# An mLSTM cell with a GELU layer behind it, on one core: the place of one weighing of values and of the sums of w_out

## The chip, the cores and the metric

The kernel runs on one core of a Trainium2 chip. A core has five engines that run side by side, each through its own list of instructions in order: TensorE (PE) multiplies matrices, VectorE (DVE), ScalarE (ACT) and GpSimd (POOL) work element by element, and SyncE (SP) issues the transfers (DMAs). An engine waits for another only where a semaphore says so. The metric is the device time of the program in microseconds; smaller is better.

## What is computed

Two blocks follow each other. The first is an mLSTM cell over 4 batches, 8 heads, 768 steps and a head dimension of 40; the second takes its result as 3072 tokens of 320 features through a hidden layer of 2048.

```python
for t in range(S):
    m_new = maximum(f[t] + m, i[t])
    C = exp(f[t] + m - m_new) * C + exp(i[t] - m_new) * outer(v[t], k[t])
    n = exp(f[t] + m - m_new) * n + exp(i[t] - m_new) * k[t]
    m = m_new
    y[t] = sigmoid(o[t]) * (C @ q[t]) / max(|n . q[t]|, 1)
x = y as (tokens, heads * head_dim)
h = x @ w_in
out = (0.5 * h * (1 + erf(h / sqrt(2)))) @ w_out
```

## The kernel before

**Chunks.** The 768 steps are cut into six chunks of 128. Within a chunk the recurrence becomes matrix products: scores of keys and queries, multiplied by a matrix W of gate weights, times the values; what comes from earlier chunks is carried in a state of each batch. A chunk of all four batches is 512 tokens, and its second block (up: x times w_in, then GELU; down: times w_out) is computed while the cell of the next chunk runs.

**Order.** The program is written out by hand as words. `FRONT` is the order of the first chunk's cell, its up and its down and of the second chunk's cell. Then a loop makes passes c = 1 to 5: `up(g, sums_too, turns)` for chunk c, and then `play(DOWN, steps)`, in which the down of chunk c (words F) and the cell of chunk c + 1 are mixed. Every engine executes its own instructions in the order in which these words issue them, so a word's place is its place in each queue. Words have a letter and a batch: M masks the weights' exponents on POOL, W takes the exponential on ACT, G is the output gate, S the scores (PE) and their product with W (DVE, line 458), C the carried part and the state's update, V the values (PE line 515), Y finishes y, X turns y for the next up (PE line 550), R splits it in two parts of fewer bits, K and Q turn keys and queries on DVE, L loads the fourth batch's blocks, Z takes the next step of a list called `later`, and N is a late sum.

**Finishing a y.** `finish(b)` (Y) multiplies the read state by the gated output on POOL (line 528) from the third chunk on, makes a denominator on DVE (lines 530 to 532), and multiplies y by its reciprocal on DVE (line 533), which needs POOL's product. The last 64 columns are then copied twice by DVE (`y_rest`, line 539) for the transposes on PE.

**Weighing values.** `weigh_values(b)` (line 442) multiplies the values of a batch by their decays. From the third chunk on it runs on POOL. It is called in `turn_q`, so directly behind the turning of the batch's queries. Only the state's update (`carry`, PE line 474) reads it.

**Down as seven products.** From the second chunk on, down is a two by two block product in Strassen's manner, in seven products instead of eight. It needs four sums of blocks of w_out: T1 = B12 - B11, T2 = B22 - T1, T3 = B22 - B12 and T4 = B21 - T2, each over 8 slices of 128x160 (`weight_sum`, line 624: one step is two subtractions on DVE). T1 and T2 lie in w_sums; T3 is written over B12 in w_out; T4 goes into three buffers that up used before. They are made once, in pass 1. The hidden layer's own sums (`hidden_sums`, lines 642 to 644) are made on DVE in each pass.

**Up.** `up` takes four pairs of hidden rows. A weight of w_in is split into a high part (ACT, line 606) and a low part (DVE, line 608), and `join_weight` (line 614) makes their difference; `split_to` and `join_weight` are no-ops once a weight is there, as in later passes. `out` is the GELU on ACT (line 725). `turns` are the K and Q of two batches of the next cell.

Of the kernel before, what the change touches and what calls it, by code (L numbers as in the profile page):

```python
# [31 lines left out]
    C2 T3 J K Y1 U U J S3 V2 C3 K J K K J J F K F F F J K J X0 K K J F R0 F F J F K G3 Y2 F J K V3 J K F K X1 J  # L32
    J R1 F F F F K X2 B8 J R2 F Y3 Z Z X3 R3 B9 B10 F"""
DOWN = """
    M0 Z M1 W0 F L3 F W1 Z Z F S0 Z S1 K2 C0 M2 Z C1 G0 G1 G2 G3 V0 Z V1 W2 Z M3 F Q2 K3 Q3 Y0 F F W3 F Z S2 S3
    C2 C3 V2 V3 F N F Y1 X0 R0 Y2 F F Y3 X1 R1 F X2 R2 F X3 R3 F"""


# [1 line left out]
def kernel(  # L40
# [18 lines left out]
    B, H, S, D = q.shape  # L59
    L = P  # L60
    NCH = S // L
# [76 lines left out]
    def load_blocks(n, to):  # L138

        c, b = divmod(n, B)  # L140
        for i, src in enumerate((k, q)):
            for d, w in ((0, 32), (32, D - 32)):
                for g in range(4):
                    t = c * L + 32 * g
                    nc.sync.dma_start(out=to[64 * i + d:64 * i + d + 32, :, 32 * g:32 * g + w],
                                      in_=src[b, :, t:t + 32, d:d + w].rearrange("h t d -> t h d"))
# [204 lines left out]
    class Cell:  # L351
# [63 lines left out]
        def turn_q(self, b):  # L415
            self.turn_half(b, 1)
            n = self.c * B + b + (1 if b < B - 2 else 2)
            if b < B - 1 and n < NCH * B:
                load_blocks(n, by_block)
            if self.c < NCH - 1:  # L420
                self.weigh_values(b)

# [171 lines left out]
    def split_weight():  # L594
        i = len(w_lo)
        if i in (0, 3, 5, 8):
            two = shared([P, NX, 2, WP // 2], F32R, "w_in_hi")
            w_hi.extend([two[:, 0], two[:, 1]])
        elif i == 2:
            two = shared([P, 2, 2, WP // 2], F32R, "w_rest_hi")  # L600
            w_hi.append(two[:, 0])
            rest_two.append(two[:, 1])
        elif i == 7:
            w_hi.append(rest_two[0])
        w = w_all[i]
        nc.scalar.activation(out=w_hi[i], in_=w, func=AF.Copy, scale=PART * 2.0 ** -12)
        w_lo.append(w_f(F32R, "w_in_lo"))
        nc.vector.scalar_tensor_tensor(out=w_lo[i], in0=w_hi[i], scalar=-BASE * 2.0 ** 12, in1=w, op0=OP.mult, op1=OP.add)
# [3 lines left out]
    def join_weight(i):  # L612
        w_mid[i] = raw.tile([P, 2, WP // 2], F32R, name="w_in_mid", tag="pow") if i % 5 in (1, 4) else w_f(F32R, "w_mid")
        nc.vector.tensor_tensor(out=w_mid[i], in0=w_hi[i], in1=w_lo[i], op=OP.add)  # L614

    def weight_sum(n):
        x, y = {1: (Bm[0][1], Bm[0][0]), 2: (Bm[1][1], T[1]), 3: (Bm[1][1], Bm[0][1])}.get(n) or (Bm[1][0], T[2])
        if n == 4:

            parts = [raw.tile([P, 3, HD], F32, name="t4", tag=tag) for tag in ("sig", "pow", "sig")]  # L620
            T[4] = lambda j: parts[j // 3][:, j % 3, :]

        def step(j):
            nc.vector.tensor_tensor(out=T[n](j), in0=x(j), in1=y(j), op=OP.subtract)

        return [lambda j=j: (step(j), step(j + 1)) for j in range(0, HF, 2)]
# [10 lines left out]
    def hidden_sums(g, f0, f1):  # L637

        (a11, a21), (_, a22) = [[g.t[:, HF * e + f0:HF * e + f1, HT * h:HT * (h + 1)] for h in range(2)]
                                for e in range(2)]  # L640
        s1, s2 = [t[f0 // (HF // 2)][:, f0 % (HF // 2):f0 % (HF // 2) + f1 - f0, :] for t in (g.s1, g.s2)]
        nc.vector.tensor_tensor(out=s1, in0=a21, in1=a22, op=OP.add)  # L642
        nc.vector.tensor_tensor(out=s2, in0=s1, in1=a11, op=OP.subtract)  # L643
        nc.vector.tensor_tensor(out=a21, in0=a11, in1=a21, op=OP.subtract)
# [44 lines left out]
    def up(g, sums_too, turns):  # L689

        def split_to(i):
            while len(w_lo) <= i:
                split_weight()

        def pair(f, ahead):

            at = [f // 2 * 5 + f % 2 * 3 + x for x in range(NX)]
            split_to(at[1])
            for i in at:
                if i not in w_mid:  # L700
                    join_weight(i)
            pus = [[pool.tile([P, TG], F32, name="pu", tag=tag) for e in range(2)]
                   for pool, tag in (((ps_h, "h"), (ps_mm, "a")), ((ps_tr, "tr"), (ps_mm, "b")))[f % 2]]
            ahead()
            mid = [w_mid.pop(i) for i in at]
            for n, (w, x) in enumerate((([w_hi[i] for i in at], parts["x"]), ([w_lo[i] for i in at], parts["x_lo"]), (mid, parts["x_all"]))):
                for i in range(2):
                    for e in range(2):
                        for k in range(NX):
                            nc.tensor.matmul(pus[i][e], w[k][:, e, i * P:(i + 1) * P], x[:, k, :],  # L710
                                             start=(n == 0 and k == 0), stop=False, skip_group_check=True)
            return pus

        def rest(u, banks, order):
            mid = w_mid.pop(5 * u + 2)
            for i in order:
                pu = banks[i]
                for n, (w, x) in enumerate(((w_hi[5 * u + 2], parts["x"]), (w_lo[5 * u + 2], parts["x_lo"]), (mid, parts["x_all"]))):
                    for e in range(2):
                        r = halves[e]  # L720
                        nc.tensor.matmul(pu[e], w[r, i // 2, i % 2 * P:(i % 2 + 1) * P], x[r, NX, :], start=False,  # L721
                                         stop=(n == 2), skip_group_check=True)

        def out(i, e, pu):
            nc.scalar.activation(out=g.t[:, HF * e + i, :], in_=pu[e], func=AF.Gelu, scale=4097.0)  # L725

        b0 = pair(0, lambda: split_to(4))
        b1 = pair(1, lambda: join_weight(2))
        for step in turns[:1]:
            step()  # L730
        rest(0, b0 + b1, (0, 1, 2, 3))
        split_to(6)
        join_weight(5)
        join_weight(6)
        for i, pu in enumerate(b0 + b1):
            for e in range(2):
                out(i, e, pu)
        b2 = pair(2, lambda: split_to(9))
        hidden_sums(g, 0, 2)
        hidden_sums(g, 2, 4)  # L740
        b3 = pair(3, lambda: join_weight(7))
        for step in turns[1:] + sums_too:
            step()
        rest(1, b2 + b3, (2, 3, 0, 1))
        for i, e in ((2, 0), (2, 1), (3, 0), (0, 0), (1, 0), (3, 1), (0, 1), (1, 1)):
            out(4 + i, e, (b2 + b3)[i])
        hidden_sums(g, HF - 2, HF)
        hidden_sums(g, HF - 4, HF - 2)
# [96 lines left out]
    def in_turn(steps):  # L845
        todo = list(steps)
        return lambda: todo.pop(0)() if todo else None

    def cell_steps(c, letters, before=None):
        cell = Cell(c)  # L850
        cell.before = before
        return dict(zip(letters, (cell.mask, cell.weights, cell.gate, cell.turn, cell.scores, cell.carry, cell.values,
                                  cell.finish, cell.turn_y, cell.split_x, cell.load_last, cell.turn_k,
                                  cell.turn_q)))

    first_g = Hidden(False)
    n_pieces = range(len(pieces))
    steps = dict(P=fetch, L=lambda n: load(n, 0, 2), O=lambda n: load(n, 2, 4), B=load_M, E=second_gates, N=later_gates,
                 I=keep_clock, D=lambda: decays_turned(0, 2, 0, 1), Q=lambda: decays_turned(2, NCH - 1, 1, NCH - 1),
                 A=in_turn(first_up_steps(0)), U=in_turn(first_up_steps(1)), F=in_turn(first_down_steps(first_g)),  # L860
                 K=in_turn(lambda i=i: conv_one(i) for i in n_pieces), H=products_begin,
                 J=in_turn(lambda i=i: conv_two(i) for i in n_pieces), Z=split_weight)
    steps |= cell_steps(0, "mwgtscvyx") | cell_steps(1, "MWGTSCVYXR")
    play(FRONT, steps)
    for c in range(1, NCH):
        g, later, steps = Hidden(True), [], {}
        if c + 1 < NCH:
            steps = cell_steps(c + 1, "MWGTSCVYXRLKQ", g)
        up(g, weight_sum(1) + weight_sum(2) if c == 1 else [], [lambda b=b: (steps["K"](b), steps["Q"](b)) for b in range(2)] if steps else [])
        if c == 1:  # L870
            later = weight_sum(3) + weight_sum(4)
        products, late = down_steps(c, g)
        steps |= dict(F=in_turn(products), Z=in_turn(later), N=late)
        play(DOWN if c + 1 < NCH else "F " * 14, steps)
# [30 lines left out]
```

## Time and profile before

| What | Value |
|---|---|
| Median of 6 runs | 491.39 us (489.97 to 494.62) |
| The profiled execution: device time | 493.81 us |
| The profiled execution: span from first to last instruction | 492.0 us |
| PE busy | 473.4 us, 96% of the span |
| DVE busy | 346.9 us, 71% |
| ACT busy | 222.8 us, 45% |
| POOL busy | 70.9 us, 14% |
| Mean granted clock of PE | 0.990 |

Times inside the profile are microseconds from the span's first instruction. An engine's timeline gives, for each group of like instructions, the start, the length of the group, the engine, the line, the operation, what it writes and reads, and how many there are; in brackets stands how long the engine sat idle before it and what ended the wait. A group's length counts from the start of its first to the end of its last instruction. Instructions of one engine can overlap by a little[...]. The stages of interest are up and down of pass 1 (135.5 to 164.5 and 164.5 to 212.1) and, for comparison, those of pass 2 (212.1 to 240.6 and 240.6 to 285.1).

### The profile page before, as it was taken

What the parts mean: (1) busy time and instruction counts of PE and PEld (TensorE: products, weight loads), DVE (VectorE), ACT (ScalarE), POOL (GpSimd) and SP (SyncE); (2) the same over time, 40 slices, a digit from 0 to 9 for tenths busy, and PEclk for the clock granted to TensorE, in tenths of its full rate; (3) what the DMA queues carried; (4) which work ended last, traced back from release to release, by engine and by line L of the source; (5) the groups of instructions that cost most, each with busy time, mean ns of one, the idle gap of its engine ahead of it and who ended that gap; (6) DMA issues with size and microseconds to landing.
All of it is one profiled execution on the core that took longest, in us unless ns stands there. A gap on an engine that the chain in (4) does not pass through costs nothing.

```text
span 492.0 us, 10730 instructions
## 1 busy us (share of the span) xinstructions
PE 473.4 (96%) x4184; PEld 412.8 (84%) x4184; DVE 346.9 (71%) x727; ACT 222.8 (45%) x477; POOL 70.9 (14%) x108
## 2 busy tenths in 40 slices
PE   3899999999999998999999999999999999999997
PEld 2687888877677898987899987899987899977996
DVE  7689787989877997956577856487857387724321
ACT  7595999845434762113672113672103762212300
POOL 3001120000100125400035400036000113000000
PEclk9599999999999999999999999999999999999999
DMA  6979954338561246832237932246931240000001
GB/s 115 238 182 197 243 124 95 104 108 179 105 152 14 31 87 107 168 80 28 27 61 130 172 87 22 28 84 110 177 82 20 31 87 8 28 27 1 1 0 55
DMA packets 164434, 44.24 MB, mean 90 GB/s; under 512 B 154176, under 2 KB 157408, under 8 KB 164384
## 3 DMA queue, kind: packets, MB, share of 16 engines
q1 hardware_dynamic: 164384, 43.56, 45.0%
q8 instruction: 33, 0.54, 0.5%
q14 instruction: 17, 0.14, 0.1%
HBM read 39.52 MB, written 4.01 MB: 88 GB/s over the span
## 4 chain that ended last, share of the span: by engine, by line
PE 80%; DVE 9%; ACT 4%; DMA 2%; issue 2%; POOL 1%; SPq 0%; DVEq 0%; POOLq 0%
PE po L784 28%; PE pu L710 21%; PE po L761 7%; PE pu L721 6%; PE pu L655 4%; PE ps L455 4%; PE ph L515 3%; PE pf L479 2%; PE pf L474 1%; ACT W L390 1%; PE px L550 1%; PE pu L661 1%; DMA bits<-in_moe_w_in_dram 1%; DMA W<-M_d 1%; DVE ob L533 1%
## 5 line engine op out<-in xcount | busy, mean ns | idle before, releaser
L784 PE MATMUL po<-w_out,g 128*128 128x160 f32 x640 | 91.2, 300 | 0.0
L725 ACT ACTIVATE g<-pu 128x512 f32<-128x512 f32 x80 | 40.8, 614 | 108.1 <-PE pu L721 108.0
L784 PEld LDWEIGHTS po<-w_out,g 128*128 128x128 f32 x640 | 87.8, 190 | 1.8 <-ACT g L725 1.8
L390 ACT ACTIVATE W<-W,aT 128x128 f32<-128x128 f32 x160 | 48.8, 389 | 3.6 <-POOL W L364 3.5
L784 PE MATMUL po<-w_sums,sums 128*128 128x160 f32 x320 | 47.5, 302 | 0.0
L784 PEld LDWEIGHTS po<-w_sums,sums 128*128 128x128 f32 x320 | 44.2, 190 | 0.7 <-DVE sums L643 0.3
L560 ACT ACTIVATE x_hi<-px 128x384 fp32r<-128x384 f32 x20 | 9.8, 490 | 75.8 <-PE px L550 75.8
L458 DVE TENSOR_TENSOR W<-ps,W 128x512 f32<-128x512 f32 x48 | 30.2, 682 | 17.1 <-ACT W L390 11.8
L710 PE MATMUL pu<-x_hi,w_in_hi 128*128 128x512 f32 x160 | 41.4, 401 | 0.0
L710 PE MATMUL pu<-x_lo,w_in_lo 128*128 128x512 f32 x160 | 40.6, 395 | 0.0
L364 POOL TENSOR_SCALAR_AFFINE_SELECT W<-W 128x1024 f32<-128x1024 f32 x20 | 22.6, 1135 | 103.5 <-DMA W<-M_d 92.4
L642 DVE TENSOR_TENSOR sums<-g 128x512 f32<-128x512 f32 x20 | 13.8, 688 | 33.3 <-ACT g L725 33.3
L710 PEld LDWEIGHTS pu<-x_hi,w_in_hi 128*128 128x128 f32 x160 | 29.4, 188 | 8.2 <-ACT g L725 1.9
L710 PEld LDWEIGHTS pu<-x_lo,w_in_lo 128*128 128x128 f32 x160 | 30.1, 188 | 7.2
L761 PE MATMUL po<-w_out,g 128*128 128x320 f32 x128 | 35.7, 434 | 0.0
L710 PE MATMUL pu<-x_all,w_in_mid 128*128 128x512 f32 x80 | 31.7, 396 | 0.1
L710 PE MATMUL pu<-x_all,w_mid 128*128 128x512 f32 x80 | 31.7, 396 | 0.0
L761 PEld LDWEIGHTS po<-w_out,g 128*128 128x128 f32 x128 | 23.8, 190 | 9.3
L797 DVE TENSOR_TENSOR o_sb<-po,o_sb 128x320 f32<-128x320 f32 (+1 forms) x27 | 12.5, 464 | 26.9 <-PE po L784 23.0
L614 DVE TENSOR_TENSOR w_in_mid<-w_in_hi,w_in_lo 128x512 fp32r<-128x512 f32 x20 | 14.6, 732 | 21.6 <-PE pu L710 21.6
L655 PE MATMUL pu<-first_x,w_in 128*128 128x256 f32 x128 | 28.8, 381 | 0.5 <-DVE W L458 0.5
L402 POOL MEMSET g<- 32x1024 f32 x8 | 7.6, 945 | 148.1 <-ACT W L390 117.6
(166 smaller groups left out, 882.9 us busy)
## 6 DMA issues: line engine op xcount, KB each, us to landing
W<-M_d SPq DMA_DIRECT2D x20, 512.0 KB, 5.3
bits<-in_moe_w_in_dram SPq DMA_DIRECT2D x20, 256.0 KB, 5.0
bits<-in_moe_w_out_dram SPq DMA_DIRECT2D x16, 320.0 KB, 3.1
ob<-in_o_gate_dram SPq DMA_DIRECT2D x24, 160.0 KB, 3.8
out_dram<-o_sb SPq DMA_DIRECT2D x24, 160.0 KB, 1.9
vb<-in_v_dram SPq DMA_DIRECT2D x22, 160.0 KB, 5.4
kb<-in_k_dram SPq DMA_DIRECT2D x22, 160.0 KB, 5.0
blocks<-in_k_dram SPq DMA_DIRECT2D x48, 32.0 KB, 2.2
```

The costliest lines, as they stand in the source:

```text
L364: nc.gpsimd.affine_select(out=t, in_=t, compare_op=OP.is_ge, fill=1.0e30, base=0, pattern=[[0, H], [1, L]], channel_multiplier=-1)
L390: nc.scalar.activation(out=W[n][:, h, :], in_=src, func=AF.Exp, scale=-1.0, bias=aT[:, self.c, r:r + 1])
L455: nc.tensor.matmul(ps[hip][:, p, :], kT[r, p, :], qT[r, p, :], start=True, stop=True)
L458: nc.vector.tensor_tensor(out=w, in0=ps[hip], in1=w, op=OP.mult)
L515: nc.tensor.matmul(ph[r, h, :], Pm[:, h, r], vb[turn_of(n)][:, h, :], start=True, stop=True)
L614: nc.vector.tensor_tensor(out=w_mid[i], in0=w_hi[i], in1=w_lo[i], op=OP.add)
L655: nc.tensor.matmul(banks[-1][e][:, i - i0, :], in_tile(i, x)[:, e, i % 2 * P:(i % 2 + 1) * P], first_x[:, x, t0:t1], start=(x == 0 and i = ...
L710: nc.tensor.matmul(pus[i][e], w[k][:, e, i * P:(i + 1) * P], x[:, k, :], start=(n == 0 and k == 0), stop=False, skip_group_check=True)
L721: nc.tensor.matmul(pu[e], w[r, i // 2, i % 2 * P:(i % 2 + 1) * P], x[r, NX, :], start=False, stop=(n == 2), skip_group_check=True)
L725: nc.scalar.activation(out=g.t[:, HF * e + i, :], in_=pu[e], func=AF.Gelu, scale=4097.0)
L761: nc.tensor.matmul(po[b], g.t[:, f, b * L:(b + 1) * L], w_out[:, f, :], start=(f == 0), stop=(f == NF - 1))
L784: nc.tensor.matmul(bank[at][:, i, :], lhs(j, t), rhs(j), start=(first and i == 0 and j == 0), stop=(i == n - 1 and j == HF - 1), skip_grou ...
```

## The change

It has two parts.

The first takes the fourth batch's `weigh_values(3)` out of `turn_q` and gives it a word of its own, D3, which stands in `DOWN` behind Y0, the finishing of the first y. On POOL, the weighing of the fourth batch's values and the multiplication of the first y change places. This concerns passes 1, 2 and 3; the cell of the last chunk weighs nothing.

The second moves the sums of w_out in pass 1. Before, T1 and T2 (8 steps, 16 subtractions) were made in `up`, behind the turning of the second batch's keys and queries, and T3 and T4 (8 steps) in the words Z of `DOWN`. Now five steps (all of T1 and the first of T2) stand ahead of the third pair of hidden rows, directly behind the GELUs of the first two pairs; the other three steps of T2 and the four of T3 stand where T1 and T2 stood; and only T4's four steps are left for the words Z, of which they take the first four. The number of instructions of each kind stays the same on every engine.

```diff
 DOWN = """
-    M0 Z M1 W0 F L3 F W1 Z Z F S0 Z S1 K2 C0 M2 Z C1 G0 G1 G2 G3 V0 Z V1 W2 Z M3 F Q2 K3 Q3 Y0 F F W3 F Z S2 S3
+    M0 Z M1 W0 F L3 F W1 Z Z F S0 Z S1 K2 C0 M2 Z C1 G0 G1 G2 G3 V0 Z V1 W2 Z M3 F Q2 K3 Q3 Y0 D3 F F W3 F Z S2 S3
...
             if b < B - 1 and n < NCH * B:
                 load_blocks(n, by_block)
+            if self.c < NCH - 1 and b < B - 1:
+                self.weigh_values(b)
+
+        def weigh_last(self, b):
             if self.c < NCH - 1:
                 self.weigh_values(b)
...
                 out(i, e, pu)
+        for step in sums_too[:5]:
+            step()
         b2 = pair(2, lambda: split_to(9))
         hidden_sums(g, 0, 2)
         hidden_sums(g, 2, 4)
         b3 = pair(3, lambda: join_weight(7))
-        for step in turns[1:] + sums_too:
+        for step in turns[1:] + sums_too[5:]:
             step()
...
-            steps = cell_steps(c + 1, "MWGTSCVYXRLKQ", g)
-        up(g, weight_sum(1) + weight_sum(2) if c == 1 else [], [lambda b=b: (steps["K"](b), steps["Q"](b)) for b in range(2)] if steps else [])
+            steps = cell_steps(c + 1, "MWGTSCVYXRLKQD", g)
+        up(g, weight_sum(1) + weight_sum(2) + weight_sum(3) if c == 1 else [], [lambda b=b: (steps["K"](b), steps["Q"](b)) for b in range(2)] if steps else [])
         if c == 1:
-            later = weight_sum(3) + weight_sum(4)
+            later = weight_sum(4)
```

## The prediction

> **What bounds the kernel now.** The page's table of engines has TensorE (PE) busy for 473.4 of 492.0 us, and 80% of the chain that ended last is PE: a change pays only where PE waits. So I asked next for the busy time by stage. The windows view, cut where the chain shows PE passing from up to down, gives for pass 1 (two rows, up and down) and pass 2 (two rows), in columns stretch, PE, weight loads, VectorE (DVE), ScalarE (ACT), GpSimd (POOL), clock, DMA share, GB/s:
>
> ```profile
> 135.50:164.50 29.00, 28.89 (x146) 21.98 (x144) 23.23 (x39) 11.96 (x22) 1.10 (x1) 1.00 0.35 72
> 164.50:212.10 47.60, 45.51 (x557) 43.94 (x558) 41.64 (x98) 21.14 (x50) 16.97 (x22) 1.00 0.62 111
> 212.10:240.60 28.50, 28.50 (x146) 22.01 (x144) 16.16 (x25) 6.05 (x12) 0.00 (x0) 1.00 0.23 34
> 240.60:285.10 44.50, 44.50 (x559) 43.82 (x558) 34.33 (x72) 21.18 (x51) 16.84 (x22) 1.00 0.64 114
> ```
>
> Pass 2's down does the same matmuls in 44.5 us with PE never idle; pass 3 is the same (44.4). Pass 1's takes 47.6, and DVE is 7.3 us busier there: mainly 16 of the 32 subtractions that make the sums of w_out. By the chain's starts the stages are 47.65 (164.48 to 212.13) and 44.45 (240.63 to 285.08): **3.20 us is all that pass 1's down can give back**, and the later passes can give nothing.
>
> The timeline of PE shows where the 3.20 lies (start, length, instruction, idle before it):
>
> ```profile
> 191.56 0.32 PE L515 MATMUL ph<-vb,W 128*64 128x41 f32 x4 [0.91 <-DVE W L458]
> 192.16 2.21 PE L515 MATMUL ph<-vb,W 128*64 128x41 f32 x60 [0.28 <-DVE W L458]
> 207.12 0.33 PE L550 MATMUL px<-ident,y_rest 128*128 128x128 f32 x1 [0.81 <-DVE y_rest L539]
> ```
>
> Part by part against pass 2, from the chain: to the second pair of scores 21.96 against 21.67, 0.29 more (the waits list it as po L784 for sums L643, 0.3); scores to the end of values (ph) 7.93 against 6.05, **1.88** more (two rows above); ph to the next up 17.76 against 16.73, 1.03 more (third row and the restart). Sum 3.20.
>
> Why DVE is late for W, in the timelines of DVE and POOL:
>
> ```profile
> 178.11 0.56 DVE L624 TENSOR_TENSOR t<-w_out,w_sums 128x160 f32<-128x160 f32 x2
> ...
> 189.11 0.49 DVE L533 TENSOR_TENSOR ob<-ob,den 128x320 f32<-128x320 f32 x1 [2.00 <-POOL ob L528]
> 189.63 0.23 DVE L539 COPY y_rest<-ob 128x128 f32<-128x128 f32 x1
> 189.78 1.12 DVE L624 TENSOR_TENSOR t<-w_out,w_sums 128x160 f32<-128x160 f32 x2
> 190.82 2.47 DVE L458 TENSOR_TENSOR W<-ps,W 128x512 f32<-128x512 f32 x4
> ```
>
> ```profile
> 185.89 0.74 POOL L442 TENSOR_TENSOR vw<-vb,ewT 128x328 f32<-128x328 f32 x1
> 187.58 0.74 POOL L442 TENSOR_TENSOR vw<-vb,ewT 128x328 f32<-128x328 f32 x1 [0.95 <-DMA vb<-in_v_dram]
> 188.27 0.81 POOL L528 TENSOR_TENSOR ob<-far,ob 128x320 f32<-128x320 f32 x1
> ```
>
> Two causes: POOL weighs the fourth batch's values (second vw), waits 0.95 us for their DMA, and only then multiplies the first y that DVE stands waiting for; and DVE carries subtractions between its other work.
>
> **D3, the fourth batch's values behind the first y.** POOL runs the same instructions, two of them swapped, in passes 1, 2 and 3; SyncE's queue and its DMAs keep their order. The y multiply (ob L528) has its inputs from 180.2 on (far L523), so it follows the first vw: 186.65 to 187.46 instead of 188.27 to 189.08, 1.62 us earlier. The moved vw waits for its DMA until 187.58 anyway, so it loses nothing here; in pass 2 it slips from 262.30 to about 262.65, in pass 3 by 0.8 to about 335.3. Behind it on POOL stand the state decays, which wait for PE (189.70, 265.56, 338.52), and on PE the fourth carry (about 189.2, 265.3, 338.3): 2.6 us of cover or more in passes 2 and 3, 0.9 in pass 1. Cost nothing.
>
> Here a rule weighs against it. The Trainium skill, page "SBUF — State Buffer", section "SBUF: two separate sides", says that DVE with two SBUF inputs and GpSimd reading SBUF lock each other out for the whole of an instruction. The moved vw now runs beside DVE's L533, which it did not before. The nearest row is pass 4, whose POOL already goes straight into ob and runs a second one beside L533:
>
> ```profile
> 407.72 1.08 DVE L533 TENSOR_TENSOR ob<-ob,den 128x320 f32<-128x320 f32 x1 [0.56 <-POOL ob L528]
> ```
>
> 1.08 instead of 0.49. By the row L533 loses 0.6, by the rule at most one vw, 0.74; without either, nothing. I take 0.7. Pass 1: L533 starts at 187.5, ends by 188.7; y_rest to 188.9; the first two W products (0.62 each) are ready at 190.15. PE, undisturbed, asks at 164.48 + 25.88 (pass 2's distance, 266.51 - 240.63) = 190.36. So D3 alone, with the two T4 subtractions at 189.78 out of the way, just covers the 1.88. In passes 2 and 3 DVE gets 0.5 us of margin that PE doesn't need: 0.
>
> **Ten subtractions into DVE's gap in up.** T1's eight and T2's first two now stand ahead of the third pair's weights:
>
> ```profile
> 148.69 0.68 DVE L614 TENSOR_TENSOR w_in_mid<-w_in_hi,w_in_lo 128x512 fp32r<-128x512 f32 x1
> 152.20 0.69 DVE L608 SCALAR_TENSOR_TENSOR w_in_lo<-w_rest_hi,w_rest 128x512 fp32r<-128x512 f32 x1 [2.82 <-ACT w_rest_hi L606]
> ...
> 162.97 1.97 DVE L624 TENSOR_TENSOR w_sums<-w_out 128x160 f32<-128x160 f32 x8
> 164.87 1.96 DVE L624 TENSOR_TENSOR w_sums<-w_out,w_sums 128x160 f32<-128x160 f32 x8
> ```
>
> The gap is 149.37 to 152.20, 2.83 us: DVE waits for w_rest_hi, which ACT does after eight gelus. Sixteen subtractions ran from 162.97 to 166.75, 0.236 each, so ten take 2.36: hidden, 0.47 to spare, POOL idle. w_out has long been converted (the last conversion ends at 129.5). If the cover were gone it would be paid one for one: this DVE work leads through the hidden sums to w_mid at 158.26, for which PE waits at 159.6. The second rule: page "VectorE: DVE Perf Modes", section "The TRN2 errata", prices an fp32 tensor_tensor at (N+151)/0.96, for N = 160 an estimate of 324 ns, and asks for tiles of 512 elements or more. That is also what a single one lasts in the trace (median 317), but back to back they start every 236. By the rule's duration ten would take 3.24 and put 0.41 on the path; by the row 0. I take the row, as it is the same instruction.
>
> **Fourteen behind the transposes of the second y's keys, T3 out of down.** In their place were sixteen: 14 x 0.236 = 3.30 instead of 3.78, so the last hidden sums come 0.48 earlier, and with them the end of the 0.29 wait, the clearing of g on POOL (170.83, released by DVE g L644) and SyncE's queue of block loads behind it, hence the mask of the fourth weights. T3 overwrites columns of w_out that only the earlier down and T1 read, both done. In down T4's eight take the places of T3's eight (six before the first W product, which waits for PE anyway; one of the eight waits for a buffer that PE last reads at 161.4), and T4's old places (0.56 + 0.47 + 0.47 + 1.04 = 2.5 us of DVE time from 178.1 to 190.8) fall empty. This doubles the cover of D3: the DVE chain then starts its den by about 184.8 instead of 186.5, and POOL is what ends last there.
>
> **The tail, 1.03.** PE waits at 206.3 for y_rest, since DVE's L531 and L533 took 1.00 and 1.03 (0.17 and 0.49 in pass 2) beside POOL's vw and masks, whose start at 203.64 a DMA sets. With PE and DVE about 2.2 us earlier and SyncE's queue only 0.5, that POOL work falls after the chain, as in pass 2 (y_rest 10.7 us after ph, vw 10.7, masks 11.4). I take all 1.03; bounds 0 and 1.03.
>
> **Sum.** 0.29 + 1.88 + 1.03 = 3.2 us. The profiled execution (493.81, of which the span is 492.0) would become 490.6. It lies 2.4 us above the runs' median; I take the same microseconds off that: 491.39 - 3.2 = **488.2 us**, its own range 487.4 to 488.9.
>
> **Rivals.**
> - *The tail stays*: POOL's masks still meet the den chain. For it: their start hangs on a DMA; against: 0.9 us of margin. Gain 2.17: 489.2.
> - *The stalls are the profiled execution's*: it is 2.4 us slower than the median, and if that lies in these waits only 0.8 is left: 490.6. Against it: the DVE backlog is fixed work, and a profile lengthens the whole.
> - *Slower: subtractions at twice the price.* The pair at 189.78 took 0.52 each beside POOL. If that held in up, ten take 5.2 and put 2.37 on the path to w_mid, and fourteen take 7.28 instead of 3.78, so the sums are 3.5 later for PE; against the 2.91 still gained that is +2.96: 494.4. It decides from p where 10p - 2.83 + 14p - 3.78 = 2.91, p = 0.40 us. Against it: POOL has nothing from 140.5 to 170.8.
>
> **Chances.** 0.5% (2.46 us) is about what a measurement of this kernel can tell from no change. Forecast 0.68, tail 0.13, stalls smaller 0.10, slower 0.09. The forecast falls short of 2.46 in a few of a hundred cases: faster 0.64, same 0.27, slower 0.09. The range 487.2 to 490.6 reaches over the first two rivals.
>
> **What would show it.** Right: pass 1's down at 44.5 in the windows, no wait for W or y_rest on PE, ten L624 between 149.4 and 151.8 with L608 still at 152.2, POOL's ob ahead of the vw. Wrong: PE's wait at 159.6 grown (cover too short), a wait for y_rest left, or ph waiting for W still, with DVE held by ob.

## The result, and the profile after

The changed kernel takes 490.23 us (median of 33 runs, 489.25 to 491.07), the kernel before 491.62 us (median of 68 runs, 489.67 to 495.82). The ratio is 0.9959, with a 95% interval of 0.9946 to 0.9972: faster by 0.41%, about 2.0 us. The medians lie only 1.39 us apart and the means (492.15 and 490.12) 2.03: what went most is the upper end, since 26 of the 68 runs of before lie above 492.5 and none of the 33 of the changed kernel. The two profiled executions stand further apart: 493.81 before, 490.56 after, 3.25 us; their spans are 492.0 and 488.8. The forecast said 3.2 us for the profile and carried the same amount over to the median, 488.2, and that is 2.0 below the measured one.

The windows view of the changed kernel, cut at its own stages (up and down of pass 1, then of pass 2; columns as before):

```profile
135.50:164.50 29.00, 28.90 (x146) 22.00 (x144) 24.64 (x49) 11.95 (x22) 1.64 (x1) 1.00 0.35 73
164.50:208.90 44.40, 44.40 (x557) 43.72 (x558) 38.58 (x88) 21.14 (x51) 15.81 (x22) 1.00 0.61 104
208.90:237.40 28.50, 28.50 (x146) 22.01 (x144) 16.15 (x25) 6.03 (x12) 0.00 (x0) 1.00 0.33 57
237.40:281.90 44.50, 44.50 (x559) 43.82 (x558) 34.21 (x72) 21.20 (x51) 15.81 (x22) 1.00 0.63 113
```

In the second row TensorE is busy for all of the 44.40 us, where before it had 45.51 in 47.60. Pass 1's down is now as long as pass 2's, though DVE still has 4 us more to do in it (38.58 against 34.21).

The timelines of DVE, then of POOL, then of PE, at the places that the forecast named:

```profile
149.31 1.97 DVE L628 TENSOR_TENSOR w_sums<-w_out 128x160 f32<-128x160 f32 x8
151.19 0.55 DVE L628 TENSOR_TENSOR w_sums<-w_out,w_sums 128x160 f32<-128x160 f32 x2
152.21 0.69 DVE L612 SCALAR_TENSOR_TENSOR w_in_lo<-w_rest_hi,w_rest 128x512 fp32r<-128x512 f32 x1 [0.47 <-ACT w_rest_hi L610]
...
186.66 1.01 DVE L537 TENSOR_TENSOR ob<-ob,den 128x320 f32<-128x320 f32 x1 [0.54 <-POOL ob L532]
...
187.84 2.47 DVE L462 TENSOR_TENSOR W<-ps,W 128x512 f32<-128x512 f32 x4
...
202.09 0.49 DVE L537 TENSOR_TENSOR ob<-ob,den 128x320 f32<-128x320 f32 x1
```

```profile
185.12 0.74 POOL L446 TENSOR_TENSOR vw<-vb,ewT 128x328 f32<-128x328 f32 x1
185.81 0.81 POOL L532 TENSOR_TENSOR ob<-far,ob 128x320 f32<-128x320 f32 x1
186.58 0.74 POOL L446 TENSOR_TENSOR vw<-vb,ewT 128x328 f32<-128x328 f32 x1
```

```profile
190.19 2.01 PE L519 MATMUL ph<-vb,W 128*64 128x41 f32 x64
...
203.99 0.27 PE L554 MATMUL px<-ident,y_rest 128*128 128x128 f32 x1
```

Lines 628, 612, 532, 537, 462, 446, 519 and 554 here are 624, 608, 528, 533, 458, 442, 515 and 550 of the kernel before. The ten subtractions fill DVE's gap with 0.47 us left of it; the first y comes off POOL at 186.62 instead of 189.08, 0.84 earlier than forecast, mostly since the mask ahead of both weighings (POOL line 364) starts at 184.06 instead of 184.83; the W products begin at 187.84 instead of 190.82; the last denominator's multiplication takes 0.49 again instead of 1.03; and PE has no wait left at either place. So every part of the forecast is visible in this execution. What is left to explain is why the timed runs show less.

### The profile page after: what moved, and what is told of

It reads as the page before. It is cut to its first block, busy times and chain, and to the rows that moved or that the text cites. A ratio compares the mean times of both kernels' runs of the same rounds, so it can differ in the third digit from the quotient of the medians.

```text
span 488.8 us, 10729 instructions
## 1 busy us (share of the span) xinstructions
PE 472.8 (97%) x4184; PEld 413.2 (85%) x4184; DVE 345.0 (71%) x727; ACT 222.8 (46%) x477; POOL 68.6 (14%) x108
## 4 chain that ended last, share of the span: by engine, by line
PE 89%; DVE 5%; ACT 4%; DMA 1%; issue 1%; SPq 0%; DVEq 0%; ACTq 0%
PE po L790 32%; PE pu L714 21%; PE po L767 7%; PE pu L725 6%; PE pu L659 5%; PE ps L459 5%; PE ph L519 5%; PE pf L483 2%; PE pf L478 2%; PE px L554 1%; PE pu L665 1%; ACT g L729 1%; PE pt L433 1%; DVE M L218 1%; DMA bits<-in_moe_w_in_dram 1%
```

## Experiments

Two theories stood against each other. A: the runs of the kernel before differ among themselves in the waits of pass 1's down, because the first y waits on POOL behind a transfer of values, and the profiled execution was one of the long ones. B: the runs differ elsewhere (ahead of pass 1), and the gain is lost in another way. All stage lengths below are read in one manner, from the start of TensorE's first matmul of a stage in the timeline to the start of the next stage's (this gives 47.45 for pass 1's down before, where the chain gave 47.65, and 44.25 where the expectations say 44.5; up reads 29.27 where they say 28.94; the differences are the same). "vw wait" is what POOL waited for the transfer ahead of the fourth values; "y" is when POOL starts the first y, counted from the start of down.

| Kernel (profiled execution) | span | up | down | y | vw wait | runs timed |
|---|---|---|---|---|---|---|
| before, first profile | 492.0 | 29.27 | 47.45 | 23.86 | 0.95 | 489.67 to 495.82 |
| before again (n1) | 490.0 | 29.31 | 45.45 | 22.02 | 0 | 490.27 to 494.85 |
| before, third (n8) | 490.6 | 29.27 | 46.46 | 23.45 | 0.75 | one |
| values there (n5) | 487.6 | 29.29 | 44.82 | 22.50 | 0 | 489.37 to 492.29 |
| D3 alone (n2) | 489.7 | 29.31 | 44.86 | 21.78 | 0 | 489.48 to 493.02 |
| sums alone (n3) | 491.6 | 29.27 | 46.93 | 23.91 | 1.46 | 489.17 to 493.39 |
| changed | 488.8 | 29.27 | 44.25 | 21.39 | 0 | 489.25 to 491.07 |
| changed again (n7) | 487.7 | 29.28 | 44.25 | 21.48 | 0.19 | 489.46 to 490.85 |
| changed, beside n9 (n10) | 487.6 | 29.29 | 44.25 | 21.46 | 0 | 489.36 to 491.33 |
| gap overfilled (n4) | 488.8 | 30.16 | 44.25 | 21.08 | 0 | 490.02 to 491.53 |
| sums behind pair (n6) | 489.4 | 28.85 | 44.64 | 21.97 | 0.77 | 490.79 to 492.54 |
| pass 1 only (n9) | 488.0 | 28.84 | 44.25 | 21.85 | 0.75 | 488.96 to 491.11 |

**The kernel before, profiled twice more.** No edit.

> The kernel before, profiled once more, for its spread. Theory A (its runs differ in the waits of pass 1's down, because the first y on GpSimd waits for a transfer of values that lands at a different time each run): pass 1's down is not 47.65 us again but between 45 and 49, the span of the profile differs by the same amount, and every other stage keeps its length within 0.2 us. Theory B (the runs differ elsewhere, in the first 135 us, and the profiled execution was a usual one): pass 1's down is 47.4 to 47.9 again, and a longer or shorter span comes from the stages before 135.5 us.

> A third profile of the kernel before. Theory A: pass 1's down is 45.6 us where GpSimd's second vw follows the first at once, and 1.5 to 2.5 us longer where it waits for its transfer, and the span moves with it. Theory B: the length of that stage does not follow that wait.

Measured: n1 492.54 us (median of 12; ratio to before 1.0015, 0.9988 to 1.0041). The 35 other runs of this same kernel on that chip have a median of 491.51, so medians of 12 runs of before can lie 1.0 us apart with no change at all. The down of pass 1 is 2.00 us shorter than in the first profile, and the span is 2.0 us shorter; up is the same to 0.04. In the third profile down is 0.99 shorter. POOL of the first profile, then of n1, then of n8:

```profile
184.83 1.09 POOL L364 TENSOR_SCALAR_AFFINE_SELECT W<-W 128x1024 f32<-128x1024 f32 x1 [6.87 <-DMA W<-M_d]
```

```profile
184.01 1.09 POOL L364 TENSOR_SCALAR_AFFINE_SELECT W<-W 128x1024 f32<-128x1024 f32 x1 [6.00 <-DMA W<-M_d]
185.07 1.48 POOL L442 TENSOR_TENSOR vw<-vb,ewT 128x328 f32<-128x328 f32 x2
186.51 0.81 POOL L528 TENSOR_TENSOR ob<-far,ob 128x320 f32<-128x320 f32 x1
```

```profile
185.35 0.74 POOL L442 TENSOR_TENSOR vw<-vb,ewT 128x328 f32<-128x328 f32 x1
186.84 0.74 POOL L442 TENSOR_TENSOR vw<-vb,ewT 128x328 f32<-128x328 f32 x1 [0.75 <-DMA vb<-in_v_dram]
187.53 0.81 POOL L528 TENSOR_TENSOR ob<-far,ob 128x320 f32<-128x320 f32 x1
```

In n1 the two weighings follow each other at once, because the values have landed. Three profiles of one kernel stand in the order of that wait: 0, 0.75 and 0.95 us give 45.45, 46.46 and 47.45. That is theory A's direction in each. The 45.6 and the 1.5 to 2.5 more that A expected of the third hold for 0.95 but not for 0.75, where 1.01 more was seen. The wait is not all of it: counted from the start of down, the first y of the first profile is 1.84 us later than n1's, 0.95 by this wait and 0.90 by the mask ahead of it, which itself waited for a transfer (184.83 - 164.41 = 20.42 against 184.01 - 164.49 = 19.52). So two transfers stand ahead of the first y, and D3 takes away one. In all three profiles one wait stays: TensorE waits 0.69, 0.80 and 0.81 us for y_rest near the end of down. The row of n1:

```profile
205.21 0.33 PE L550 MATMUL px<-ident,y_rest 128*128 128x128 f32 x1 [0.69 <-DVE y_rest L539]
```

**The wait for the values taken away.** The kernel before, but the fourth batch's weighing reads the third batch's values, so the fourth batch's carried state is another one.

```diff
-            self.engine.tensor_tensor(out=vw, in0=vb[turn_of(self.c * B + b)],
+            self.engine.tensor_tensor(out=vw, in0=vb[turn_of(self.c * B + b - (1 if self.c > 1 and b == B - 1 else 0))],
```

> The kernel before, in which the weighing of the fourth batch's values reads the third batch's values instead, which have landed by then: the instruction stays in its place, only its wait for the transfer is gone (the states of the fourth batch come out different). Theory A (before's runs differ because that transfer lands late in some): GpSimd's two vw follow each other at once, the wait for W on TensorE is 0 to 0.9 us in the profile, no run above 492.5, a median of 490.5 to 491.2. Theory B (the wait is in the profile only, or another transfer makes the spread): as before in median (491.4 to 492.6) and in spread (up to 494 to 495).

Measured: 490.76 us, ratio 0.9979 (0.9953 to 1.0005), no run above 492.29, where the 29 runs of before on that chip reach 495.54 and 11 of them lie above 492.5. Down is 44.82. The order of instructions, the subtractions and the place of the first y are those of before; only what the weighing waits for has changed, and the long runs are gone. POOL:

```profile
184.17 1.43 POOL L442 TENSOR_TENSOR vw<-vb,ewT 128x328 f32<-128x328 f32 x2
185.56 0.81 POOL L528 TENSOR_TENSOR ob<-far,ob 128x320 f32<-128x320 f32 x1
```

This is theory A with its numbers. The ratio's interval just touches 1, so the gain in time is less sure than the cut of the spread. That down is 0.63 shorter here than in n1 is not the edit's doing as far as can be seen: PE doesn't wait for y_rest here, because POOL's weighing near the end of down (held by its own transfer) starts 39.74 us after the start of down, behind the last multiplication of DVE line 533 (38.90), where in n1 it starts at 38.55, ahead of that multiplication (38.62).

**Each part alone.** D3 without the sums, and the sums without D3. The first is the changed kernel with these lines taken back; the second is the kernel before with the second part of the change alone.

```diff
-        for step in sums_too[:5]:
-            step()
...
-        for step in turns[1:] + sums_too[5:]:
+        for step in turns[1:] + sums_too:
...
-            later = weight_sum(4)
+            later = weight_sum(3) + weight_sum(4)
```

> D3 alone, the sums of w_out as before. The first y comes off GpSimd some 1.6 us earlier, but two of T4's subtractions (1.0 us) still stand between it and the W products, and VectorE's backlog stays. Theory A: the wait for W on TensorE shrinks from 1.88 to 0.6 to 0.9 us, the 0.29 stays, pass 1's down is 45.4 to 46.3 us; timed 0.2 to 0.4% faster than before, and the slow end of the runs (493 to 496) is gone, since no transfer of values stands ahead of the first y. Theory B (the sums carry it all): pass 1's down stays within 0.4 us of before's, and so does the time.

> The sums moved, the weighing of the fourth values still ahead of the first y. VectorE is some 1.7 us earlier at the first y, but GpSimd ends it as before, by the transfer of values. Theory A: no 0.29, a wait for W of 0 to 0.5 us where the transfer lands as in the first profile, pass 1's down 44.5 to 45.3 us, the time 0.3 to 0.4% below before's, with a slow end of the runs left (above 491.5). Theory B (the sums carry it all): as the changed kernel in time and in spread (489.3 to 491.1).

Measured: D3 alone 491.11 us, ratio 0.9983 (0.9963 to 1.0003), down 44.86. The profile gains 2.6 of the 3.2, more than the 1.2 to 2.0 that A expected, since the two T4 subtractions ahead of the W products took 0.47 us and not the 1.04 of the first profile, and since the wait for y_rest went as well, as in n5 (POOL's weighing started 39.02 us after the start of down, DVE's multiplication at 38.89). In time it is at the edge of what can be told; A expected the long runs to be gone, and one of the 12 still reached 493.02. The sums alone: 490.64 us, ratio 0.9972 (0.9947 to 0.9997), down 46.93 in the profile, and runs from 489.17 to 493.39, so the long runs are still there. The profiled execution is the longest of these 12 runs. Theory B, that the sums carry it all, fails on both counts; but A, too, expected 44.5 to 45.3 for a transfer that lands as late as this one, and had no wait for y_rest in it. The profile of the sums alone says why, on POOL, on DVE and on PE:

```profile
187.59 0.74 POOL L442 TENSOR_TENSOR vw<-vb,ewT 128x328 f32<-128x328 f32 x1 [1.46 <-DMA vb<-in_v_dram]
188.28 0.81 POOL L528 TENSOR_TENSOR ob<-far,ob 128x320 f32<-128x320 f32 x1
```

```profile
189.12 0.49 DVE L533 TENSOR_TENSOR ob<-ob,den 128x320 f32<-128x320 f32 x1 [2.74 <-POOL ob L528]
```

```profile
206.56 0.33 PE L550 MATMUL px<-ident,y_rest 128*128 128x128 f32 x1 [1.14 <-DVE y_rest L539]
```

The first y starts at 188.28, in the first profile of before at 188.27. DVE comes to it earlier and waits 2.74 instead of 2.00. Work saved ahead of a wait whose end a transfer sets is only waited out. Down is still 0.52 shorter than in the first profile, by what was saved elsewhere: the wait for the sums is gone (0.29), and with no T4 subtractions between the first y and the W products these begin at 189.94 instead of 190.82, of which the longer wait for y_rest (1.14 instead of 0.81) takes back a part. The fastest run (489.17) is as fast as the changed kernel's fastest; that it is one in which the transfer was early is likely, but no profile shows it.

**The cover of the ten subtractions.** The changed kernel with all sixteen of T1 and T2 in the gap.

```diff
-        for step in sums_too[:5]:
+        for step in sums_too[:8]:
...
-        for step in turns[1:] + sums_too[5:]:
+        for step in turns[1:] + sums_too[8:]:
```

> The changed kernel with all sixteen subtractions of T1 and T2 in VectorE's gap in up, instead of ten. At 0.236 us each they take 3.78, 0.95 more than the gap of 2.83. If this VectorE work leads to the weights for which TensorE waits, as the forecast says of a missing cover, w_in_lo starts at 153.1 to 153.2 instead of 152.2, TensorE's wait at 159.6 grows by 0.9 to 1.0, and the kernel is about 0.9 us (0.2%) slower than the changed one. If the path has slack, nothing changes.

Measured: 491.09 us, 0.9 above the changed kernel's 490.23, which was measured on another chip; the surer figure is the stage, up 30.16 instead of 29.27, 0.89 more. The kernel's first part ran 1.35 us earlier in this execution, so 151.74 below stands for 153.09. DVE, then TensorE:

```profile
149.85 1.97 DVE L628 TENSOR_TENSOR w_sums<-w_out,w_sums 128x160 f32<-128x160 f32 x8
151.74 0.69 DVE L612 SCALAR_TENSOR_TENSOR w_in_lo<-w_rest_hi,w_rest 128x512 fp32r<-128x512 f32 x1
```

```profile
158.54 0.50 PE L714 MATMUL pu<-x_all,w_mid 128*128 128x512 f32 x1 [0.67 <-DVE w_mid L618]
```

The idle time ahead of w_in_lo is gone and TensorE waits for w_mid. The gap of 2.83 us is real room, and of the 0.95 us past it 0.89 were paid, as the forecast said of a missing cover.

**Trying to win what is left of up.** Pass 1's up is 0.4 us longer than the others', because hidden sums stand ahead of w_mid on DVE. First they are moved behind the fourth pair in all passes.

```diff
-        hidden_sums(g, 0, 2)
-        hidden_sums(g, 2, 4)
         b3 = pair(3, lambda: join_weight(7))
+        hidden_sums(g, 0, 2)
+        hidden_sums(g, 2, 4)
```

> The changed kernel with the first four hidden sums of each up behind the weights of the fourth pair instead of ahead of them. In pass 1 the six additions (3.86 us) no longer stand between w_in_lo and w_mid, so w_mid is ready by about 156.3 instead of 158.9 and TensorE's fourth pair waits for nothing: up 28.5 to 28.6 us instead of 28.94, 0.35 to 0.45 us (0.08%) less in the profile, at the edge of what the timed runs can tell. If the sums come too late for the second product, TensorE waits there instead and nothing or less is gained.

Measured: 491.2 us, ratio 0.9966 (0.9944 to 0.9988), where the changed kernel on the same chip has 489.87 and 0.9959: slower by the medians, not told apart by the ratios. Up falls to 28.85 as expected, but 0.39 comes back in down, where the second product waits for its sums, and the down of pass 4 loses 0.7 (43.18 instead of 42.46). SyncE's queue in pass 4, of the changed kernel, then of this one:

```profile
377.46 3.77 SPq L145 DMA_DIRECT2D blocks<-in_k_dram  x8
...
398.17 0.38 SPq L160 DMA_DIRECT2D W<-M_d  x1
```

```profile
381.25 3.76 SPq L145 DMA_DIRECT2D blocks<-in_k_dram  x8
...
399.15 0.38 SPq L160 DMA_DIRECT2D W<-M_d  x1
```

The turning of queries now stands behind the sums on DVE, the loads of blocks that it releases start 3.8 us later, and the transfer for the fourth weights, at the end of that queue, 1.0 later; POOL's mask of these weights then starts at 403.23 instead of 402.58. So the move costs where up has nothing to win. The next kernel makes it in pass 1 alone, and puts T3's subtractions behind the last hidden sums.

```diff
+        early = lambda: (hidden_sums(g, 0, 2), hidden_sums(g, 2, 4))
+        if not sums_too:
+            early()
         b3 = pair(3, lambda: join_weight(7))
-        for step in turns[1:] + sums_too[5:]:
+        if sums_too:
+            early()
+        for step in turns[1:] + sums_too[5:8]:
...
         hidden_sums(g, HF - 4, HF - 2)
+        for step in sums_too[8:]:
+            step()
```

> The changed kernel with two more moves in pass 1 alone: the first four hidden sums behind the fourth pair's weights, and T3's eight subtractions behind the last hidden sums instead of ahead of them, so that the sums for the second product are 1.9 us earlier. Pass 1's up falls from 28.94 to 28.5 us and its down stays at 44.5, later passes stay as they are: 0.4 us below the changed kernel in the profile's stages, 0.1% in time, less than the two groups of its runs lie apart. If VectorE's time is needed in pass 1's down after all, a wait for W comes back and the gain is lost.

> The changed kernel beside the one above, on the same chip: up 28.9 and down 44.5 us in pass 1, runs between 489.2 and 491.1 in two groups, 0.3 to 0.5% below before.

Measured: 489.96 us, ratio 0.9954 (0.9931 to 0.9977); the changed kernel beside it 490.29, ratio 0.9964 (0.9944 to 0.9985). Up is 28.84 and down 44.25, so the 0.4 us is there in the profile; in time the two can't be told apart. POOL of this kernel also shows what D3 is for:

```profile
185.54 0.81 POOL L532 TENSOR_TENSOR ob<-far,ob 128x320 f32<-128x320 f32 x1
187.10 0.74 POOL L446 TENSOR_TENSOR vw<-vb,ewT 128x328 f32<-128x328 f32 x1 [0.75 <-DMA vb<-in_v_dram]
```

The same 0.75 us of waiting that came with 1.01 us more of down in n8 costs nothing here: the first y is done before it.

**The changed kernel once more.**

> The changed kernel once more, beside the others on one chip. Theory A (it no longer hangs on the transfer of values): every run between 489.2 and 491.2, in two groups about 1 us apart as in its first runs, pass 1's down 44.5 us in the profile whenever that transfer lands, and 0.2 to 0.4% below before. Theory B (its first profile was a lucky one): a wait for W or y_rest on TensorE shows up, and runs above 491.5.

Measured: 489.87 us, ratio 0.9959 (0.9936 to 0.9982), all runs between 489.46 and 490.85, down 44.25 for the second time.

## Why the prediction was right, and where it was not

- *3.20 us is all that pass 1's down can give back*: right for the profile. 47.45 became 44.25, in three profiles of the changed kernel alike.
- *D3 costs nothing, and L533 loses 0.7 to the lock that the Trainium skill describes in "SBUF — State Buffer", section "SBUF: two separate sides"*: right in kind, and 0.52 in size: L533 (now L537) took 1.01 beside the moved vw at 186.58 instead of 0.49. The row of pass 4 (1.08) had told the same. It depends on which of the two starts first: in n9, where the vw came after it, L537 took 0.49, and in n7, where L537 started at 185.51 and the vw at 185.67, L537 kept its 0.49 and the vw took 0.93 instead of 0.74. So an engine can be held up by another with no semaphore between them, which the first section left out. In these profiles PE didn't wait for it.
- *Ten subtractions at 0.236 are hidden, 0.47 to spare*: right to the second digit, the spare time too. The estimate of 324 ns for one, from the Trainium skill's page "VectorE: DVE Perf Modes", section "The TRN2 errata", would have used it up: it fits what one lasts in the trace (median 317), not the 236 at which they follow each other. The overfilled gap shows the price beyond: 0.89 us for 0.95 too much.
- *Fourteen bring the last sums 0.48 earlier, and the 0.29 wait goes*: right; they start at 166.29 instead of 166.75, 0.46 earlier, and the way to the second pair of scores is 21.66 instead of 21.96.
- *The tail gives back all 1.03*: right in the sum, with less room than forecast. From ph to the next up 17.49 became 16.47. The margin of 0.9 us is there in the first profile (L537 ends at 202.58, POOL's vw starts at 203.48), but in n7 and n10 that vw starts while L537 still runs, and the copy behind it takes 0.76 instead of 0.22. PE asks for it only 0.7 us later (202.55 against 201.87 in n10), so nothing is lost. Having the values of the first y in time does not bring the tail by itself: n1 keeps its wait of 0.69.
- *The sum on the profiled execution's own time, 490.6*: measured 490.56. The 3.2 us are shown; that the whole fits to 0.04 is luck in part, since both profiled executions happen to reach pass 1 at the same time (135.14 and 135.15), and two other profiled executions of the changed kernel took 489.47 and 489.39.
- *"I take the same microseconds off that: 491.39 - 3.2"*: this is the step that failed: the term of 3.2 us was read in one long execution and taken off the median whole. The waits of pass 1 are no constant of the kernel. Of the first 68 runs of before, 55 were shorter than the profiled execution's 493.81, and in n1, with the values in time, only 1.20 us of waits was there to be removed (45.45 - 44.25). The timed gain, 1.39 us by the medians and 2.0 by the ratio, lies between these ends. It is also below the 2.46 us that the forecast took for the least that can be told from no change; with 68 and 33 runs 2.0 can be told (the interval ends at 0.9972).
- *The rival "the stalls are the profiled execution's", 490.6*: it came nearest to the measured 490.23, at a chance of 0.10, and its reason is the one that the runs bear out, though its gain of 0.8 is too small. What the forecast held against it, that DVE's backlog is fixed work, was true and beside the point: the end of the wait was set by a transfer. The row for it was among the lines shown: vw waiting 0.95 us for a DMA, ahead of the y for which DVE stood still. That a profile lengthens the whole is not seen either: the profiled executions lie within the timed runs, 490.56 within 489.25 to 491.07.
- *Slower, by subtractions at twice the price*: did not happen; POOL had nothing to do from 141.1 to 170.4, while the twenty-four ran.

What stays open is why the values land late in some runs and not in others. In all three profiles of before SyncE's queue issues its loads without a pause from 170.9 us to the load of these values. Part of the lateness is in the queue: the loads of blocks ahead took 5.45 us to issue in the first profile and 4.81 in n1, so that the values' load was issued 16.68 and 16.02 us after the start of down; the rest came between issue and landing (6.49 us in the first profile, at most 5.3 in n1). No experiment moved that load. That the longest runs of before (above 495 us) lie so far out for the same reason is likely from n5, where they are gone, but no profile caught one.

## What to carry to other kernels

Set the profiled execution's own time against the spread of the timed runs before its waits are counted as gain: if it lies high among them and a wait ends with a transfer, the wait is worth less in the median than in the profile. An instruction that waits for a transfer should not stand ahead of one that another engine is waiting for, even when the transfer lands in time in most runs; in this kernel moving it cut most of the long runs, and work saved ahead of the wait was waited out. Fill a gap only as far as it reaches: here 0.95 us past its end cost 0.89.

## What was not expected

The runs of the changed kernel still spread over 1.8 us (489.25 to 491.07), in two loose groups. Its profiles with spans of 487.6 and 487.7 reach pass 1's up at 133.7 to 133.9 us, the one of 488.8 at 135.15, so this difference lies in the first chunk. Theory B is thus right for this part of the spread. TensorE's timeline of the first of these (n10), then of the changed kernel's first profile:

```profile
21.64 0.39 PE L385 MATMUL pm<-M_parts,row 96*128 96x128 bf16 x4
```

```profile
22.73 0.63 PE L385 MATMUL pm<-M_parts,row 96*128 96x128 bf16 x4
```

The same four small matmuls take 0.39 us in one and 0.63 in the other, and in the slower one this lasts until about 24 us. The row of granted clock does not tell it: it says 1.00 from 10 to 25 us in the slower one and 0.50 from 15 to 20 in the quicker one. What makes TensorE reach its pace earlier in some runs is not settled here. Both are seen with the old order too (n5 reaches up at 133.77, n1 at 135.18), and the change touches nothing ahead of pass 1.
